# Token tiles of 480 columns in place of 416 in an attention and two-MLP kernel

## The chip, the core and the metric

The kernel runs on one core of a Trainium2 chip. The metric is the device time of one execution in microseconds (us), as the median of three runs. The engines are named as the profile names them: PE (TensorE, the matmuls), PEld (its weight loads, which run beside the matmuls), DVE (VectorE), ACT (ScalarE), POOL (GpSimd) and SP (SyncE, which issues most DMAs).

## The reference, cut to what matters

There are N = 12480 tokens of C = 128 channels and m = 32 inducing points. Two attentions follow each other, and then two MLPs with a hidden width of 2048. The outer function is the last one.

```python
def mab(q, kv):
    s = scale * (q @ kv.transpose(0, 2, 1))
    s = s - s.max(-1, keepdims=True)
    a = np.exp(s)
    a /= a.sum(-1, keepdims=True) + 1e-09
    return a @ kv
h = mab(I, x)
return mab(x, h).astype(np.float32)
...
h = x @ w_in
g = np.maximum(h, 0.0) + alpha * np.minimum(h, 0.0)
return (g @ w_out).astype(np.float32)
...
h = np.maximum(x @ w_in, 0.0)
return (h * h @ w_out).astype(np.float32)
```

`I` are the 32 inducing rows, which attend to all tokens; then each token attends to the 32 rows of `h`, and its result goes through the first MLP and the second, each 128 to 2048 to 128.

## The kernel before

**Stages.** The first attention reads all tokens once in its own tiles of 512 (`TILE1`) and a rest of 192; it needs every token before its result `hT` exists. Behind it the tokens are cut anew into `NT` = 30 tiles of `T` = 416. A tile is a matrix with channels (or 32 x 4 rows) on the partitions and its tokens on the columns, so every matmul behind the first attention has 416 moving columns, and every evacuation by ACT, DVE or POOL works on 128x416.

**Second attention.** `second_attention(tiles)` makes the softmax weights of the tokens for four tiles at once: the scores by four small matmuls (L449) side by side in one bank, then transposes, maximum, exponential and sum, and at the end a split into a rounded part and its remainder that DMAs spread over the partitions of `a_s`. Tile 0 goes alone, and its 416 tokens are cut into four pieces of 128 that overlap (`cuts`); tiles 1 to 3 come next, and from tile 4 on groups of four, with a last group of two. The steps of a group begin two tiles ahead of its first tile.

**Main loop.** A step `s` stands for one tile and one of 16 chunks of 128 hidden units; there are `total` = NT x 16 = 480 of them. In a step PE does ten matmuls in the reduced fp32 format (fp32r): `l1_a` one (L590, first MLP in; the attention's values are folded into the weights `w1s`), `l1_b` three (first MLP out; L600 to L602 are the three lines of the helper `three`, rounded and remainder parts), `l2_a` three (second MLP in) and `l2_b` three (second MLP out). `end_y1` adds one more matmul (L617) per tile. Each matmul has its own weight load. ACT evacuates `l1_a` (L594), `l2_a` (L632) and rounds the square (L640); DVE makes the remainder of the first (L596) and the square (L634); POOL makes the remainder of the square (L642), which DVE does in the last `LAG2` = 24 steps.

**Lags and fill.** `l1_b` runs 3 to 5 steps behind `l1_a`, `l2_a` 24 steps, `l2_b` 28 steps. So steps 0 to 23 hold only `l1_a` and `l1_b`. Into steps 0 to 40 the table `plan` and the list `PIECES` put the work that prepares weights: the inputs are 64-bit floats that come as pairs of 32-bit words and are turned into fp32 by ACT (L183, L186), DVE (L190, L194) and POOL (L195), then split into rounded and remainder parts (ACT L219 and L234, POOL L200), and a product of weights (`step_u`, 32 fp32 matmul records of 128 columns, L565).

**Order.** The instructions of an engine run in the order in which the code writes them; nothing is rearranged. What sets a step's work is the step number, never the width of a tile.

```python
    for s in range(total + LAG2 + LAG2B + 4):
        if s < total:
            l1_a(s, s < LAG2 and s % 2)
        if 0 <= s - LAG2 < total:
            l2_a(s - LAG2)
        if 0 <= s - LAG2 - 1 < total:
            l2_split(s - LAG2 - 1)
        ends = [(l1_b, i) for i in l1_b_at.get(s, [])]
```

Of the kernel before, what the change touches and what calls it, by code (L numbers as in the profile page):

```python
# [9 lines left out]
F32 = mybir.dt.float32  # L10
F32R = mybir.dt.float32r
I32 = mybir.dt.int32
U32 = mybir.dt.uint32
AF = mybir.ActivationFunctionType
ALU = mybir.AluOpType
AX = mybir.AxisListType


T = 416


TILE1 = (512, 128, 4)
# [2 lines left out]
Q = 4  # L25
# [3 lines left out]
def attention_then_two_mlps(ctx: ExitStack, tc, x, inducing, w_in, w_out, alpha, w2_in, w2_out, out):  # L29
# [15 lines left out]
    tiles1 = [(i * TILE1[0], *TILE1) for i in range(n1)] + [(n1 * TILE1[0], *REST1)]
# [3 lines left out]
    att = ctx.enter_context(tc.tile_pool(name="att", bufs=1))  # L49
# [7 lines left out]
    h2_bank = lambda: bank("h2", 2)  # L57
# [15 lines left out]
    f32 = lambda ap: ap.bitcast(F32)  # L73
# [40 lines left out]
    xT = keep_tile("xT", [P, N])  # L114

    def xt_cols(t):
        return xT[:, t * T : (t + 1) * T]

    w1s = keep_tile("w1s", [P, DFF], F32R)
    wo_hi = keep_tile("wo_hi", [P, NCH, P], F32R)  # L120
# [78 lines left out]
    def pool_lo(lo, a, hi):  # L199
        nc.gpsimd.tensor_tensor(lo, a, f32(hi), op=ALU.subtract)  # L200
# [155 lines left out]
    b = free_bank()  # L356
# [80 lines left out]
    def second_attention(tiles, cuts=None):  # L437

        nt = Q if cuts else len(tiles)
        n, w = nt * M, P if cuts else T
        v = {}

        def step_scores():
            b = v["s"] = free_bank()
            for i in range(nt):
                rhs = xt_cols(tiles[0])[:, cuts[i] : cuts[i] + w] if cuts else xt_cols(tiles[i])
                nc.tensor.matmul(  # L449
                    b[i * M : (i + 1) * M, :w], hT[:, :M], rhs, start=True, stop=True,  # L450
                    tile_position=(0, i * M),
                )

        def step_transpose():
            a = v["a"] = att.tile([P, T // M, M], F32, name="a2", tag="a2")
            v["a"] = a[:n, : w // M]
            nc.vector.transpose(a[:n].rearrange("p b j -> p (b j)")[:, :w], v["s"][:n, :w])

        def step_max():
            a = v["a"]  # L460
            mx = att.tile([P, T // M], F32, name="mx", tag="mx")[:n, : w // M]
            nc.vector.reduce_max(mx, a, axis=AX.X)
            nc.vector.tensor_tensor(a, a, mx.unsqueeze(2).to_broadcast([n, w // M, M]), op=ALU.subtract)

# [12 lines left out]
        def step_back():
            t = v["t"] = att.tile([P, T], F32, name="a2t", tag="a2t")
            nc.vector.transpose(t[:n, :w], v["a"].rearrange("p b j -> p (b j)"))

        def new_a_s(t):
            a_s[t] = att.tile([P, T], F32R, name="a_s", tag="a_s", bufs=5)
            return a_s[t]

        def step_split():

            hi = att.tile([P, T], F32R, name="a_hi", tag="a_hi")
            nc.scalar.copy(hi[:n], v["t"][:n])
            lo = att.tile([P, T], F32R, name="a_lo", tag="a_lo")
            pool_lo(lo[:n], v["t"][:n], hi[:n])  # L490
            for i, t in enumerate(tiles):
                d = new_a_s(t)
                for k in range(4):
                    nc.sync.dma_start(
                        out=f32(d[k * M : (k + 1) * M, :]),
                        in_=f32((lo if k % 2 else hi)[i * M : (i + 1) * M, :]),
                    )

        def step_spread():
            b = v["b"] = y1_bank()  # L500
            for i in range(nt):
                skip = max(0, cuts[i - 1] + w - cuts[i]) if i else 0
                nc.tensor.matmul(
                    b[:, cuts[i] + skip : cuts[i] + w], same_q[:, i, :], v["t"][:, skip:w], start=True, stop=True
                )

        def step_split_spread():

            d = a_s[tiles[0]] = new_a_s(tiles[0])[: 3 * M]
            nc.scalar.copy(d, v["b"][: 3 * M, :T])  # L510
            lo = d[M : 2 * M]
            nc.vector.tensor_tensor(lo, v["b"][M : 2 * M, :T], f32(lo), op=ALU.subtract)

        steps = [step_scores, step_transpose, step_max, step_exp, step_sum, step_back]
        return steps + ([step_spread, step_split_spread] if cuts else [step_split])
# [12 lines left out]
        else:  # L528
            nc.scalar.copy(dst, b)

    first = second_attention([0], [0, P, 2 * P, T - P])
    second = second_attention([1, 2, 3])
    first[0]()
    make_w1s(0)
# [51 lines left out]
    def l1_a(i, other_bank):  # L586
        t, c = divmod(i, NCH)
        b = h2_bank() if other_bank else h1_bank()
        a = a_s[t]
        nc.tensor.matmul(b[:, :T], w1s[: a.shape[0], c * P : (c + 1) * P], a, start=True, stop=True)  # L590

        tag = "g2" if i < EARLY and i % 2 else "g1"
        hi = wk.tile([P, T], F32R, name="g1h", tag=tag + "h", bufs=4)
        nc.scalar.activation(hi, b[:, :T], AF.Relu)  # L594
        lo = wk.tile([P, T], F32R, name="g1l", tag=tag + "l", bufs=4)
        nc.vector.scalar_tensor_tensor(lo, b[:, :T], 0.0, f32(hi), op0=ALU.max, op1=ALU.subtract)  # L596
        g1[i] = hi, lo

    def three(b, w_hi, w_lo, hi, lo, start, stop):
# [4 lines left out]
    def l1_b(i):  # L604
        t, c = divmod(i, NCH)
        if c == 0:
            y1_cur[t] = y1_bank() if t != 1 else y2_bank()
        b = y1_cur[t][:, :T]
        hi, lo = g1.pop(i)
        three(b, wo_hi[:, c, :], wo_lo[:, c, :], hi, lo, c == 0, False)  # L610
        if c == NCH - 1 and t:
            end_y1(t)

    def end_y1(t):
        b = y1_cur.pop(t)[:, :T]
        a = a_s.pop(t)
        nc.tensor.matmul(b, v_s[: a.shape[0]], a, start=False, stop=True)  # L617
        hi = wk.tile([P, T], F32R, name="y1h", tag="y1h", bufs=2)
        nc.scalar.copy(hi, b)  # L619
        lo = wk.tile([P, T], F32R, name="y1l", tag="y1l", bufs=2)  # L620
        nc.vector.tensor_tensor(lo, b, f32(hi), op=ALU.subtract)  # L621
        y1_split[t] = hi, lo

    def l2_a(i):
        t, c = divmod(i, NCH)
        b = h2_bank()[:, :T]
        cols = slice(c * P, (c + 1) * P)
        three(b, w2[0][:, cols], w2[1][:, cols], *y1_split[t], True, True)
        if c == NCH - 1:
            del y1_split[t]  # L630
        r = wk.tile([P, T], F32, name="r", tag="r", bufs=2)
        nc.scalar.activation(r, b, AF.Relu)  # L632
        sq = wk.tile([P, T], F32, name="sq", tag="sq", bufs=3)
        nc.vector.tensor_tensor(sq, b, r, op=ALU.mult)  # L634
        rr[i] = sq

    def l2_split(i):
        sq = rr.pop(i)
        hi = wk.tile([P, T], F32R, name="g2h", tag="g2h", bufs=4)
        nc.scalar.copy(hi, sq)  # L640
        lo = wk.tile([P, T], F32R, name="g2l", tag="g2l", bufs=4)
        (nc.vector if i >= total - LAG2 else nc.gpsimd).tensor_tensor(lo, sq, f32(hi), op=ALU.subtract)  # L642
        g2[i] = hi, lo

    def l2_b(i):
        t, c = divmod(i, NCH)
        if c == 0:
            y2_cur[t] = y2_bank()
        b = y2_cur[t][:, :T]
        hi, lo = g2.pop(i)  # L650
        cols = slice(c * P, (c + 1) * P)
        three(b, w2[2][:, cols], w2[3][:, cols], hi, lo, c == 0, c == NCH - 1)
        if c == NCH - 1:

            o = wk.tile([P, T], F32, name="o", tag="o", bufs=2)
            nc.vector.transpose(o, b)
            del y2_cur[t]
            dst = out[t * T : (t + 1) * T, :].rearrange("(b i) (a j) -> a i b j", i=M, j=M)
            for a in range(P // M):

                (nc.scalar if t == NT - 1 and a % 2 else nc.sync).dma_start(
                    out=dst[a], in_=o[a * M : (a + 1) * M, :].rearrange("i (b j) -> i b j", j=M)
                )
# [120 lines left out]
```

## Time and profile before

| | |
|---|---|
| time, median of 3 runs | 984.76 us (984.51 to 985.15) |
| span of the profiled execution, first to last instruction | 983.3 us |
| what lies around the span, against the median | 1.5 us |
| PE busy | 969.8 us (99%) |
| ACT busy | 769.2 us (78%) |
| DVE busy | 683.7 us (70%) |
| POOL busy | 555.3 us (56%) |
| mean granted TensorE clock | 0.995 of full speed |

The span is that of one execution taken by the profiler; the three times are of other executions. The busy share of PE is that of records that overlap, since a matmul begins before the one ahead of it has ended: what one matmul costs in a stream is the distance from its start to the next start.

### The profile page before, as it was taken

To read this page: it belongs to the slowest core of one execution; us is meant where nothing else is said; L and a number is where in the kernel's file an instruction comes from. 1 tells how busy PE (TensorE), PEld (TensorE's weight loads), DVE (VectorE), ACT (ScalarE), POOL (GpSimd) and SP (SyncE) were. 2 spreads that over 40 slices of the span, in tenths; PEclk is the share of its full clock that TensorE was granted. 3 is DMA by queue.
4 is the path that set the end of the run, shared out by engine and by line. 5 is a ranking of instruction groups with operands and counts; after the bars stand their busy time and mean duration, and the time that the engine had idled before them with its cause. 6 is when DMAs were issued, how large, how long until landed. Compare 5 with 4: busy or idle time off the path is not lost.

```text
span 983.3 us, 16104 instructions
## 1 busy us (share of the span) xinstructions
PE 969.8 (99%) x5353; PEld 941.0 (96%) x5353; DVE 683.7 (70%) x1204; ACT 769.2 (78%) x1600; POOL 555.3 (56%) x518
## 2 busy tenths in 40 slices
PE   9899999999999999999999999999999999999998
PEld 7578999999999999999999999999999999999997
DVE  5788876667766677666776667766677666766667
ACT  5689887778877787777787777877778777787776
POOL 2358865555655556555565555655556555565530
PEclk9989999999999999999999999999999999999999
DMA  9422001000010000100001000110001000010001
GB/s 331 146 90 66 10 11 34 10 10 10 14 31 10 10 9 17 29 10 10 9 19 27 10 9 10 25 21 10 9 9 29 17 10 10 10 27 1 10 9 19
DMA packets 66356, 28.42 MB, mean 29 GB/s; under 512 B 54224, under 2 KB 62176, under 8 KB 66272
## 3 DMA queue, kind: packets, MB, share of 16 engines
q1 hardware_dynamic: 65408, 27.28, 11.2%
q8 instruction: 42, 0.69, 0.3%
q14 instruction: 42, 0.34, 0.1%
q10 hardware_dynamic: 864, 0.11, 0.1%
HBM read 14.80 MB, written 6.39 MB: 22 GB/s over the span
## 4 chain that ended last, share of the span: by engine, by line
PE 93%; DVE 2%; ACT 2%; DMA 1%; issue 0%; SPq 0%; ACTq 0%; DVEq 0%
PE y L602 18%; PE y L601 18%; PE y L600 18%; PE h L602 9%; PE h L600 9%; PE h L601 9%; PE h L590 9%; DMA xg<-in_x_dram 1%; PE h L259 1%; ACT g1h L594 1%; PE ms L449 1%; PE y L617 1%; DVE g1l L596 0%; PE ms L273 0%; ACT aw L216 0%
## 5 line engine op out<-in xcount | busy, mean ns | idle before, releaser
L642 POOL TENSOR_TENSOR g2l<-sq,g2h 128x416 fp32r<-128x416 f32 x456 | 496.7, 1090 | 343.8 <-ACT g2h L640 208.0
L596 DVE SCALAR_TENSOR_TENSOR g1l<-h,g1h 128x416 fp32r<-128x416 f32 x480 | 282.5, 589 | 221.0 <-ACT g1h L594 216.3
L594 ACT ACTIVATE g1h<-h 128x416 fp32r<-128x416 f32 x480 | 248.3, 518 | 133.2 <-PE h L590 130.1
L634 DVE TENSOR_TENSOR sq<-h,r 128x416 f32<-128x416 f32 x480 | 283.5, 591 | 51.5 <-ACT r L632 5.0
L632 ACT ACTIVATE r<-h 128x416 f32<-128x416 f32 x480 | 249.1, 519 | 54.2 <-PE h L602 8.5
L640 ACT CAST g2h<-sq 128x416 fp32r<-128x416 f32 x480 | 255.3, 532 | 1.5 <-DVE sq L634 1.3
L590 PE MATMUL h<-a_s,w1s 128*128 128x416 f32 (+1 forms) x480 | 171.0, 358 | 3.1 <-DVE g1l L596 1.8
L602 PE MATMUL y<-g2l,w2o_hi 128*128 128x416 f32 x480 | 168.6, 351 | 0.0
L602 PE MATMUL y<-g1l,wo_hi 128*128 128x416 f32 x480 | 168.4, 351 | 0.0
L600 PE MATMUL h<-y1h,w2i_hi 128*128 128x416 f32 x480 | 168.0, 350 | 0.3 <-ACT y1h L619 0.2
L602 PE MATMUL h<-y1l,w2i_hi 128*128 128x416 f32 x480 | 167.9, 350 | 0.1
L601 PE MATMUL h<-y1h,w2i_lo 128*128 128x416 f32 x480 | 168.0, 350 | 0.0
L601 PE MATMUL y<-g1h,wo_lo 128*128 128x416 f32 x480 | 168.0, 350 | 0.0
L601 PE MATMUL y<-g2h,w2o_lo 128*128 128x416 f32 x480 | 167.9, 350 | 0.0
L600 PE MATMUL y<-g1h,wo_hi 128*128 128x416 f32 x480 | 167.8, 350 | 0.0
L600 PE MATMUL y<-g2h,w2o_hi 128*128 128x416 f32 x480 | 167.5, 349 | 0.0
L590 PEld LDWEIGHTS h<-a_s,w1s 128*128 128x128 f32 (+1 forms) x480 | 90.7, 189 | 12.0 <-DVE g1l L596 5.7
L600 PEld LDWEIGHTS h<-y1h,w2i_hi 128*128 128x128 f32 x480 | 90.0, 188 | 2.8 <-DVE sq L634 1.3
L600 PEld LDWEIGHTS y<-g1h,wo_hi 128*128 128x128 f32 x480 | 90.5, 188 | 1.0 <-issue 0.5
L601 PEld LDWEIGHTS y<-g2h,w2o_lo 128*128 128x128 f32 x480 | 90.1, 188 | 0.9 <-POOL w2o_lo L200 0.4
L601 PEld LDWEIGHTS y<-g1h,wo_lo 128*128 128x128 f32 x480 | 90.4, 188 | 0.5
L602 PEld LDWEIGHTS h<-y1l,w2i_hi 128*128 128x128 f32 x480 | 90.0, 188 | 0.7 <-DVE y1l L621 0.5
(124 smaller groups left out, 757.0 us busy)
## 6 DMA issues: line engine op xcount, KB each, us to landing
out_dram<-o SPq DMA_DIRECT2D x118, 52.0 KB, 1.9
xg<-in_x_dram SPq DMA_DIRECT2D x10, 512.0 KB, 9.3
raw<-in_moe_w_in_dram SPq DMA_DIRECT2D x8, 512.0 KB, 6.1
raw<-in_moe_w_out_dram SPq DMA_DIRECT2D x8, 512.0 KB, 4.1
a_s<-a_hi SPq DMA_DIRECT2D x58, 52.0 KB, 1.9
a_s<-a_lo SPq DMA_DIRECT2D x58, 52.0 KB, 1.9
xg<-in_x_dram SPq DMA_DIRECT2D x4, 256.0 KB, 3.5
out_dram<-o ACTq DMA_DIRECT2D x2, 52.0 KB, 2.4
```

The costliest lines, as they stand in the source:

```text
L259: nc.tensor.transpose(b[:, k * p : (k + 1) * p], x_t[g][:p, i, k, :], ident[:p, :p])
L449: nc.tensor.matmul(b[i * M : (i + 1) * M, :w], hT[:, :M], rhs, start=True, stop=True, tile_position=(0, i * M),)
L590: nc.tensor.matmul(b[:, :T], w1s[: a.shape[0], c * P : (c + 1) * P], a, start=True, stop=True)
L594: nc.scalar.activation(hi, b[:, :T], AF.Relu)
L596: nc.vector.scalar_tensor_tensor(lo, b[:, :T], 0.0, f32(hi), op0=ALU.max, op1=ALU.subtract)
L600: nc.tensor.matmul(b, w_hi, hi, start=start, stop=False)
L601: nc.tensor.matmul(b, w_lo, hi, start=False, stop=False)
L602: nc.tensor.matmul(b, w_hi, lo, start=False, stop=stop)
L632: nc.scalar.activation(r, b, AF.Relu)
L634: nc.vector.tensor_tensor(sq, b, r, op=ALU.mult)
L640: nc.scalar.copy(hi, sq)
L642: (nc.vector if i >= total - LAG2 else nc.gpsimd).tensor_tensor(lo, sq, f32(hi), op=ALU.subtract)
```

## The change

Behind the first attention the tokens are cut into 26 tiles of 480 instead of 30 of 416; both make 12480. The tile widths stand in a list `WIDTHS`, and every place that used `T` takes the width of its tile. The first attention keeps `TILE1`. The number of steps becomes 26 x 16 = 416; the lags, `plan` and `PIECES` keep their step numbers. Tile 0 of the second attention is cut at 0, 128, 256 and 352 instead of 0, 128, 256 and 288.

```diff
-T = 416
+WIDTHS = [(26, 480)]
+T = max(w for _, w in WIDTHS)
...
-    assert N % T == 0
-    NT = N // T
+    assert sum(n * w for n, w in WIDTHS) == N
+    wide = [w for n, w in WIDTHS for _ in range(n)]
+    first_token = [sum(wide[:t]) for t in range(len(wide) + 1)]
+    NT = len(wide)
...
-    groups = [list(range(a, min(a + Q, NT))) for a in range(0, NT, Q)]
+    groups, t = [], 0
+    for n, _ in WIDTHS:
+        groups += [list(range(a, min(a + Q, t + n))) for a in range(t, t + n, Q)]
+        t += n
...
-        return xT[:, t * T : (t + 1) * T]
+        return xT[:, first_token[t] : first_token[t + 1]]
...
-    first = second_attention([0], [0, P, 2 * P, T - P])
+    first = second_attention([0], [0, P, 2 * P, wide[0] - P])
...
-        a = a_s[t]
-        nc.tensor.matmul(b[:, :T], w1s[: a.shape[0], c * P : (c + 1) * P], a, start=True, stop=True)
+        a, w = a_s[t], wide[t]
+        nc.tensor.matmul(b[:, :w], w1s[: a.shape[0], c * P : (c + 1) * P], a, start=True, stop=True)
...
-        b = y1_cur[t][:, :T]
+        b = y1_cur[t][:, : wide[t]]
...
-            dst = out[t * T : (t + 1) * T, :].rearrange("(b i) (a j) -> a i b j", i=M, j=M)
+            dst = out[first_token[t] : first_token[t + 1], :].rearrange("(b i) (a j) -> a i b j", i=M, j=M)
```

On every engine the instructions keep their order; they become wider, and the later part of the program has fewer of them. On PE, where the main loop begins, these are the rows of before (L503 spreads the weights of tile 0 over the partitions, L590 is `l1_a`, L522 makes the weights `w1s`):

```order
L449 MATMUL ms<-xT,hT 32x416 x3
L389 MATMUL y_687<-ident,w_in_sb 128x128 x4
L522 MATMUL h_694<-w_in_sb,hT 128x512
L503 MATMUL y_707<-a2t,same_q 128x128 x3
L503 MATMUL y_707<-a2t,same_q 128x32
L590 MATMUL h_730<-a_s,w1s 128x416
L590 MATMUL h_741<-a_s,w1s 128x416
```

The same place on PE in the changed kernel, where the lines have moved by seven (L597 is `l1_a`):

```order
L456 MATMUL ms<-xT,hT 32x480 x3
L395 MATMUL y_687<-ident,w_in_sb 128x128 x4
L529 MATMUL h_694<-w_in_sb,hT 128x512
L510 MATMUL y_707<-a2t,same_q 128x128 x3
L510 MATMUL y_707<-a2t,same_q 128x96
L597 MATMUL h_730<-a_s,w1s 128x480
L597 MATMUL h_741<-a_s,w1s 128x480
```

No row has changed places; the fourth piece of tile 0 is 96 columns instead of 32, and the main loop's matmuls are 480 wide.

On POOL, the end of the program before (L642 is the remainder of the square, L475 and L200 belong to the last group of the second attention):

```order
L200 TENSOR_TENSOR a_lo<-a2t,a_hi 128x416
L642 TENSOR_TENSOR g2l<-sq,g2h 128x416 x56
L475 TENSOR_TENSOR a_11208<-a_11208,sm 64x416
L642 TENSOR_TENSOR g2l<-sq,g2h 128x416 x8
L200 TENSOR_TENSOR a_lo<-a2t,a_hi 64x416
L642 TENSOR_TENSOR g2l<-sq,g2h 128x416 x40
```

The same place on POOL in the changed kernel, where L652, L482 and L206 are those lines:

```order
L206 TENSOR_TENSOR a_lo<-a2t,a_hi 128x480
L652 TENSOR_TENSOR g2l<-sq,g2h 128x480 x56
L482 TENSOR_TENSOR a_9578<-a_9578,sm 64x480
L652 TENSOR_TENSOR g2l<-sq,g2h 128x480 x8
L206 TENSOR_TENSOR a_lo<-a2t,a_hi 64x480
L652 TENSOR_TENSOR g2l<-sq,g2h 128x480 x40
```

The counts of remainders between two attention steps (56, 8 and 40) are the same; ahead of this place the program has one cycle of four tiles less.

## Rows read from the trace of the kernel before

**Rows 1.** The page's first part: busy us, share of the span, instructions.

```profile
PE 969.8 (99%) x5353; PEld 941.0 (96%) x5353; DVE 683.7 (70%) x1204; ACT 769.2 (78%) x1600; POOL 555.3 (56%) x518
```

**Rows 2.** Windows: length, busy us of each engine (instructions), granted clock, DMA share, GB/s.

```profile
core 0: us, PE busy (x) PEld busy (x) DVE busy (x) ACT busy (x) POOL busy (x), PEclk, DMA share, GB/s
48.10:52.30 4.20, 2.90 (x5) 1.29 (x5) 4.08 (x7) 2.95 (x7) 3.33 (x3) 0.54 0.00 0
52.30:58.70 6.40, 6.29 (x14) 4.70 (x15) 5.90 (x12) 4.04 (x10) 2.71 (x3) 0.50 0.01 3
58.70:76.80 18.10, 17.49 (x102) 16.24 (x102) 13.71 (x24) 18.10 (x47) 10.41 (x9) 1.00 0.49 151
76.80:100.06 23.26, 22.69 (x114) 19.34 (x114) 19.29 (x33) 21.71 (x47) 21.18 (x17) 1.00 0.15 46
100.06:978.63 878.57, 878.53 (x4688) 867.84 (x4686) 608.30 (x1049) 691.56 (x1430) 503.65 (x466) 1.00 0.08 14
```

**Rows 3.** The last of these windows, the score matmuls L449 alone.

```profile
100.06:978.63 878.57, 5.42 (x44) 0.93 (x44) 1.00 0.08 14
```

**Rows 4.** Timeline of PE at 500 us, first and last of 51: start, us, instruction.

```profile
500.04 0.35 PE L590 MATMUL h<-a_s,w1s 128*128 128x416 f32 x1
...
509.42 0.35 PE L590 MATMUL h<-a_s,w1s 128*128 128x416 f32 x1
```

**Rows 5.** Timeline of PE at 57 us, where the granted clock is half.

```profile
57.39 0.55 PE L601 MATMUL y<-g1h,wo_lo 128*128 128x416 f32 x1
57.74 0.55 PE L602 MATMUL y<-g1l,wo_hi 128*128 128x416 f32 x1
58.08 0.55 PE L590 MATMUL h<-a_s,w1s 96*128 96x416 f32 x1
```

**Rows 6.** Timeline of PE, fp32 matmuls of 512 and of 128 columns.

```profile
41.39 0.59 PE L522 MATMUL h<-w_in_sb,hT 128*128 128x512 f32 x1
...
43.68 1.02 PE L522 MATMUL h<-w_in_sb,hT 128*128 128x512 f32 x2
...
66.56 1.05 PE L565 MATMUL y<-aw,wiT 128*128 128x128 f32 x8
```

**Rows 7.** Line L565: duration ns min/median/max, first and last start, form.

```profile
L565 PEld LDWEIGHTS y<-aw,wiT x32: 186/192/192, 66.4 to 72.5; 128*128 128x128 f32 x32
L565 PE MATMUL y<-aw,wiT x32: 270/275/377, 66.6 to 72.6; 128*128 128x128 f32 x32
```

**Rows 8.** Timeline of PE around the scores of one group of four tiles.

```profile
217.05 0.35 PE L602 MATMUL y<-g2l,w2o_hi 128*128 128x416 f32 x1
217.33 0.91 PE L449 MATMUL ms<-xT,hT 128*32 128x416 f32 x8
218.17 0.46 PE L590 MATMUL h<-a_s,w1s 128*128 128x416 f32 x1
218.47 0.35 PE L600 MATMUL h<-y1h,w2i_hi 128*128 128x416 f32 x1
```

**Rows 9.** The chain that ended last, 50 to 75 us: start, us, what.

```profile
50.46 1.29 DVE a L463
...
52.30 0.71 PE h L590
...
58.67 0.52 ACT g1h L594
...
74.34 0.43 ACT g1h L594
```

**Rows 10.** Groups by form, first 130 us: busy us, mean ns, idle before.

```profile
L596 DVE SCALAR_TENSOR_TENSOR g1l<-h,g1h 128x416 fp32r<-128x416 f32 x51 | 29.3, 581 | 10.1 <-ACT g1h L594 9.7
L642 POOL TENSOR_TENSOR g2l<-sq,g2h 128x416 fp32r<-128x416 f32 x25 | 28.9, 1168 | 6.4 <-ACT g2h L640 3.3 <-PE y L602 3.2
L594 ACT ACTIVATE g1h<-h 128x416 fp32r<-128x416 f32 x51 | 26.3, 524 | 5.6 <-PE h L590 5.3 <-PE y L601 0.2
...
L264 DVE COPY xT<-h 128x512 f32<-128x512 f32 x12 | 7.9, 688 | 4.0 <-PE h L259 3.8
...
L200 POOL TENSOR_TENSOR w2o_lo<-wf,w2o_hi 128x512 fp32r<-128x512 f32 x4 | 5.7, 1414 | 1.0 <-ACT w2o_hi L234 1.0
...
L529 ACT CAST w1s<-y 128x512 fp32r<-128x512 f32 x2 | 1.2, 586 | 2.0 <-PE y L522 2.0
```

**Rows 11.** Timeline of the end: last matmul and the transpose behind it.

```profile
978.14 0.45 PE L602 MATMUL y<-g2l,w2o_hi 128*128 128x416 f32 x1
978.63 0.62 DVE L656 STREAM_TRANSPOSE o<-y 128x416 f32<-128x416 f32 x1 [0.55 <-PE y L602]
```

More of the change, by code (lines that the diff above doesn't have):

```diff
@@ L441, in second_attention @@
         nt = Q if cuts else len(tiles)
-        n, w = nt * M, P if cuts else T
+        tw = wide[tiles[0]]
+        n, w = nt * M, P if cuts else tw
         v = {}
@@ L481, in new_a_s @@
         def new_a_s(t):
-            a_s[t] = att.tile([P, T], F32R, name="a_s", tag="a_s", bufs=5)
+            a_s[t] = att.tile([P, T], F32R, name="a_s", tag="a_s", bufs=5)[:, : wide[t]]
             return a_s[t]
@@ L487, in step_split @@
             hi = att.tile([P, T], F32R, name="a_hi", tag="a_hi")
-            nc.scalar.copy(hi[:n], v["t"][:n])
+            nc.scalar.copy(hi[:n, :w], v["t"][:n, :w])
             lo = att.tile([P, T], F32R, name="a_lo", tag="a_lo")
-            pool_lo(lo[:n], v["t"][:n], hi[:n])
+            pool_lo(lo[:n, :w], v["t"][:n, :w], hi[:n, :w])
             for i, t in enumerate(tiles):
@@ L494, in step_split @@
                     nc.sync.dma_start(
-                        out=f32(d[k * M : (k + 1) * M, :]),
-                        in_=f32((lo if k % 2 else hi)[i * M : (i + 1) * M, :]),
+                        out=f32(d[k * M : (k + 1) * M]),
+                        in_=f32((lo if k % 2 else hi)[i * M : (i + 1) * M, :w]),
                     )
@@ L509, in step_split_spread @@
             d = a_s[tiles[0]] = new_a_s(tiles[0])[: 3 * M]
-            nc.scalar.copy(d, v["b"][: 3 * M, :T])
+            nc.scalar.copy(d, v["b"][: 3 * M, :tw])
             lo = d[M : 2 * M]
-            nc.vector.tensor_tensor(lo, v["b"][M : 2 * M, :T], f32(lo), op=ALU.subtract)
+            nc.vector.tensor_tensor(lo, v["b"][M : 2 * M, :tw], f32(lo), op=ALU.subtract)
         steps = [step_scores, step_transpose, step_max, step_exp, step_sum, step_back]
@@ L588, in l1_a @@
         b = h2_bank() if other_bank else h1_bank()
-        a = a_s[t]
-        nc.tensor.matmul(b[:, :T], w1s[: a.shape[0], c * P : (c + 1) * P], a, start=True, stop=True)
+        a, w = a_s[t], wide[t]
+        nc.tensor.matmul(b[:, :w], w1s[: a.shape[0], c * P : (c + 1) * P], a, start=True, stop=True)
         tag = "g2" if i < EARLY and i % 2 else "g1"
[L593 to L596, printed above, removed]
+        hi = wk.tile([P, T], F32R, name="g1h", tag=tag + "h", bufs=4)[:, :w]
+        nc.scalar.activation(hi, b[:, :w], AF.Relu)
+        lo = wk.tile([P, T], F32R, name="g1l", tag=tag + "l", bufs=4)[:, :w]
+        nc.vector.scalar_tensor_tensor(lo, b[:, :w], 0.0, f32(hi), op0=ALU.max, op1=ALU.subtract)
         g1[i] = hi, lo
@@ L614, in end_y1 @@
     def end_y1(t):
-        b = y1_cur.pop(t)[:, :T]
+        w = wide[t]
+        b = y1_cur.pop(t)[:, :w]
         a = a_s.pop(t)
         nc.tensor.matmul(b, v_s[: a.shape[0]], a, start=False, stop=True)
-        hi = wk.tile([P, T], F32R, name="y1h", tag="y1h", bufs=2)
+        hi = wk.tile([P, T], F32R, name="y1h", tag="y1h", bufs=2)[:, :w]
         nc.scalar.copy(hi, b)
-        lo = wk.tile([P, T], F32R, name="y1l", tag="y1l", bufs=2)
+        lo = wk.tile([P, T], F32R, name="y1l", tag="y1l", bufs=2)[:, :w]
         nc.vector.tensor_tensor(lo, b, f32(hi), op=ALU.subtract)
@@ L625, in l2_a @@
         t, c = divmod(i, NCH)
-        b = h2_bank()[:, :T]
+        w = wide[t]
+        b = h2_bank()[:, :w]
         cols = slice(c * P, (c + 1) * P)
@@ L630, in l2_a @@
             del y1_split[t]
-        r = wk.tile([P, T], F32, name="r", tag="r", bufs=2)
+        r = wk.tile([P, T], F32, name="r", tag="r", bufs=2)[:, :w]
         nc.scalar.activation(r, b, AF.Relu)
-        sq = wk.tile([P, T], F32, name="sq", tag="sq", bufs=3)
+        sq = wk.tile([P, T], F32, name="sq", tag="sq", bufs=3)[:, :w]
         nc.vector.tensor_tensor(sq, b, r, op=ALU.mult)
@@ L638, in l2_split @@
         sq = rr.pop(i)
-        hi = wk.tile([P, T], F32R, name="g2h", tag="g2h", bufs=4)
+        w = wide[i // NCH]
+        hi = wk.tile([P, T], F32R, name="g2h", tag="g2h", bufs=4)[:, :w]
         nc.scalar.copy(hi, sq)
-        lo = wk.tile([P, T], F32R, name="g2l", tag="g2l", bufs=4)
+        lo = wk.tile([P, T], F32R, name="g2l", tag="g2l", bufs=4)[:, :w]
         (nc.vector if i >= total - LAG2 else nc.gpsimd).tensor_tensor(lo, sq, f32(hi), op=ALU.subtract)
@@ L648, in l2_b @@
             y2_cur[t] = y2_bank()
-        b = y2_cur[t][:, :T]
+        w = wide[t]
+        b = y2_cur[t][:, :w]
         hi, lo = g2.pop(i)
@@ L653, in l2_b @@
         if c == NCH - 1:
-            o = wk.tile([P, T], F32, name="o", tag="o", bufs=2)
+            o = wk.tile([P, T], F32, name="o", tag="o", bufs=2)[:, :w]
             nc.vector.transpose(o, b)
             del y2_cur[t]
-            dst = out[t * T : (t + 1) * T, :].rearrange("(b i) (a j) -> a i b j", i=M, j=M)
+            dst = out[first_token[t] : first_token[t + 1], :].rearrange("(b i) (a j) -> a i b j", i=M, j=M)
             for a in range(P // M):
```

## Prediction

> **What bounds the kernel now.** I read the page first: PE is busy 99% of the span, ACT 78%, POOL 56% [rows 1]. The windows then split the program in two at 100.06 us, the start of step 35. Behind it lie 878.6 us in which PE has no gap (878.53 of 878.57 busy) and no other engine is busy more than 79% [rows 2]. Ahead of it, from the first main-loop matmul at 48.1 us, lie 52.0 us of fill, and there the bound changes: DVE (4.08 of 4.20), then PE at half clock (6.29 of 6.40 at 0.50), then ACT (18.10 of 18.10), then a mixture in which POOL is busy 21.18 and ACT 21.71 of 23.26 us. So the change is worth two things: what a matmul costs beyond its columns in the long stage, and how far fixed work in the fill hides the wider tiles.
>
> The long stage is a pure stream. It holds 4688 PE records, 44 of them scores [rows 3], so 4644 wide matmuls. In the timeline 50 of them take 9.38 us, 187.6 ns each [rows 4]. At full clock (2.4 GHz) 416 columns are 173.3 ns. So a matmul costs some 14 ns more than its columns. At half clock the distance is 345 ns (57.39 to 58.08 for two), and 416 columns at 1.2 GHz are 346.7 ns: there the extra is gone [rows 5]. Something of about that length per matmul runs beside the columns when these are slow and sticks out when they are fast.
>
> **The change part by part: the long stage.** The columns stay what they were (12480 tokens, ten matmuls and one per tile), but the matmuls become fewer: 480 x 10 + 30 = 4830 before, 416 x 10 + 26 = 4186 after, so 644 less. All 644 go from the long stage, since the fill is the same steps: 4000 are left there.
>
> What is the extra, fixed or growing with the columns? No row shows an fp32r matmul of another width, so this is the disputed price. For fp32 matmuls two widths are there. Two records of 512 take 1.02 us, one lasts 0.59, so they start 0.43 apart, against 2 x 512 / 2.4 = 0.427; eight of 128 take 1.05, one lasts 0.275 [rows 6, 7], so the distance is 0.775 / 7 = 0.111, against 0.107. The extra is 3 to 4 ns at either width: where it can be seen at two widths, it is a price per matmul, not per column. By that I take the 14 ns as fixed. From below it is bounded by 3.5 ns fixed, the fp32 rows' own, with the rest growing by the columns, and by nothing fixed at all.
>
> The Trainium skill ("TensorE: Matmul & The Clock Gate", section "Back-to-back issue gap") gives columns / 2.4 + 2.5 ns at full clock and columns / 1.2 at half. The trace agrees at half clock (345 ns) and for the fp32 matmuls, not for the fp32r stream, which has 187.6 ns where the rule has 175.8. If only those 2.5 ns were fixed, 644 matmuls less would save 1.6 us; by my reading they save 9.3.
>
> The scores of a group of four stretch two distances from 0.38 to 1.42 us (217.05 to 218.47), so they cost 1.04 us [rows 8]; with 64 columns more in four passes (256 / 2.4 = 107 ns) 1.15. The long stage has six such groups before, five after.
>
> Before: (878.6 - 6 x 1.04 - 0.5 at the end) / 4644 = 187.7 ns, so 14.4 beyond the columns. After: 200 + 14.4 = 214.4 ns; 4000 x 0.2144 = 857.6, with 5 x 1.15 and 0.5 it is 863.8. **Term 1: -14.8 us.** The engines beside PE don't come near: a step becomes 2.14 us long, and POOL's one remainder per step about 1.33 (below).
>
> **The fill.** The same steps 0 to 34 now carry 15.4% more columns, but the conversions, the splits of the weights and the fp32 products keep their sizes. The prices of 64 columns more come from the 416-wide and the 512-wide groups of each engine [rows 10]: ACT (586 - 524) / 96 x 64 = 41 ns, DVE (688 - 581) / 96 x 64 = 71 ns, POOL (1414 - 1168) / 96 x 64 = 164 ns. These compare different operations, so they are estimates. The chain says whose time counts in each stretch: DVE to 52.3, PE to 58.7, ACT to 74 us [rows 9].
> - To 48.1: the spread and split of tile 0 stand ahead of the first L590: 64 columns more in the fourth spread, two passes each in two records (0.11), and one ACT and one DVE operation: +0.2.
> - 48.1 to 52.3: five of DVE's seven operations are 416 wide: +0.4.
> - 52.3 to 58.7, PE at half clock: 14 records, two of them 512-wide L522, so 12 x 64 / 1.2 = 53 ns: +0.6.
> - 58.7 to 76.8, ACT: steps 8 to 23 with one L594 each, and two other wide operations, 18 x 41 ns: +0.7. PE's own growth lies beneath: it has 102 records there, 34 of them fp32, and 68 x 27 ns = 1.8 us fits into its waits.
> - 76.8 to 100.06: nine of POOL's 17 operations are wide, 9 x 164 ns: +1.5. PE alone would need (114 - 8) x 0.2144 + 1.15 = 23.9, so +0.6 is the least; 15.4% of the stretch (+3.6) the most.
>
> **Term 2: +3.4 us**, between +2 and 15.4% of all 52.0 us (+8.0).
>
> **The end.** Behind the last matmul come the transpose, 0.62 us [rows 11], which grows by 0.07, and output DMAs with 15% more bytes: **+0.15**. The drain of 24 steps is part of term 1; DVE makes both its operations there, and I read its pace from the same stage, in which PE has no gap.
>
> Other edits cost nothing that shows. The second attention's operations are wider but run two tiles ahead of their use, now 32 steps of 2.14 us instead of 1.88; were that cover gone, one group's chain of some ten operations would stand open, and nothing in the long stage shows it near. There are 16 DMAs less to spread `a_s` and 16 less to the output; SP has nothing else to do by then. No step passes another on any queue, so no new wait is added; whoever waited for a 416-wide evacuation waits 40 to 160 ns longer, with lags of 3 to 5 steps around it.
>
> Sum: -14.8 + 3.4 + 0.15 = -11.2. The profiled span goes from 983.3 to 972.1; the median lies 1.5 above the span and keeps that: 984.8 - 11.2 = **973.6 us**.
>
> **The rivals.**
> - *The extra grows with the columns.* With 3.5 ns fixed a matmul takes (187.7 - 3.5) x 480 / 416 + 3.5 = 216.0 ns, 4000 of them 864.0; term 1 is -8.4 and the time 980.0. With nothing fixed, 216.6 ns: term 1 -6.0, time 982.3. For it speaks that fp32 rows show so small a fixed part, against it that the extra vanishes at half clock. The skill's rule named above, 2.5 ns fixed, falls between the two (216.2 ns).
> - *The weight load sets the pace.* PEld is busy 96% [rows 1]. If loads and columns shared one stream, 128 + 416 columns in 187.7 ns, then 128 + 480 take 209.8: 839.2, time about 955. If the load alone took 187 ns, 480 columns (203.5 with 3.5) would just pass it: time about 930. Against both: L565 has a load for each matmul and a pair every 111 ns [rows 7], and half clock shows columns alone.
> - *The clock stays low* (slower). It is about half (0.54 and 0.50) from 48.1 to 58.7 us, where PE is gappy at first and then almost without gaps [rows 2]. If it came back only behind the ACT stretch, PE would need 68 x 400 + 34 x 222 ns (twice 111) = 34.7 us there instead of the 18.8 forecast: +15.9, time about 989.5. It decides from 70% of that stretch on. Against it: PE's order is the same and its matmuls are wider, so it is busier ahead of the rise, not less.
> - *The whole fill grows as PE does*: +8.0, time 978.2, the upper end of my own case.
>
> **How the numbers follow.** My case 0.62 (its own range 972 to 978); extra that grows 0.22; load 0.08; clock 0.05; others 0.03. The range 970.5 to 983.0 takes in the first two. A measurement of this kernel tells about 0.2%, 2 us, from no change, so faster means below 982.8: nearly all of my case, the load, and most of the second, 0.84; the rest of the second, where the fill costs more than forecast, and half-way clocks: same 0.09; slower 0.07.
>
> **What would show it.** In the profile after, fifty matmuls of the long stage should take 10.72 us (10.80 to 10.83 if the extra grows, under 10.5 if the load counts). Step 35 should begin at 103.5 us, and PE's gapless stage from there last 863.8. The half clock should end near 60 us. The prediction is wrong if the distance isn't 214, or if step 35 begins beyond 108 us.

## The result and the profile after

The changed kernel takes 990.78 us (median of 4 runs, 989.65 to 991.67) against 984.92 for the kernel before in the same comparison: a ratio of 1.0056, 95% interval 1.0042 to 1.0070. It is slower by 5.9 us, where 11.2 us less was forecast. The profiled run took 989.65 us, the fastest of the four, with a span of 987.9.

The first part of the page after shows that PE is still the bound, while its loads and every other engine have more room than in [rows 1].

```profile
PE 973.2 (99%) x4701; PEld 821.2 (83%) x4701; DVE 663.6 (67%) x1061; ACT 742.5 (75%) x1402; POOL 539.8 (55%) x452
```

The windows after, cut at the same steps as [rows 2] (length, busy us of each engine with its instructions, granted clock, DMA share, GB/s):

```profile
47.80:52.09 4.29, 1.78 (x6) 0.86 (x6) 4.19 (x7) 3.08 (x7) 3.47 (x3) 1.00 0.00 0
52.09:57.43 5.34, 5.00 (x12) 3.25 (x13) 5.13 (x10) 4.15 (x9) 2.75 (x3) 0.68 0.00 0
57.43:76.89 19.46, 19.38 (x104) 16.56 (x103) 16.77 (x27) 19.04 (x47) 10.52 (x9) 1.00 0.50 147
76.89:102.51 25.62, 25.19 (x114) 19.55 (x113) 21.09 (x34) 23.66 (x48) 22.39 (x18) 1.00 0.15 42
102.51:983.00 880.49, 880.39 (x4036) 750.20 (x4034) 584.13 (x906) 661.81 (x1231) 486.59 (x399) 1.00 0.07 14
```

The last of these windows, the scores (L456) alone, answers to [rows 3]:

```profile
102.51:983.00 880.49, 5.05 (x36) 0.78 (x36) 1.00 0.07 14
```

Step 35 begins at 102.51 us, 2.45 later than before, so the fill as a whole cost less than forecast (+3.4). The long stage holds 4036 - 36 = 4000 wide matmuls, exactly the number forecast, and PE has no gap in it. But it lasts 880.5 us and not 863.8. The timeline shows why (start, us, instruction; first and last of 51, as in [rows 4]):

```profile
500.77 0.38 PE L597 MATMUL h<-a_s,w1s 128*128 128x480 f32 x1
...
511.69 0.38 PE L597 MATMUL h<-a_s,w1s 128*128 128x480 f32 x1
```

Fifty matmuls take 10.92 us, 218.4 ns each, where 214.4 was forecast. Over the stage it is (880.4 - 5 x 1.15 - 0.5) / 4000 = 218.5 ns, 18.5 beyond the 200 ns of the columns instead of 14.4. That is 4.1 ns x 4000 = 16.4 us, nearly the whole miss of 17.2. The new distance is more than 480 / 416 times the old one (216.6): between these two kernels the extra neither stayed fixed nor grew in step with the columns, it grew faster.

### The profile page after: what moved, and what is told of

Its sections match the earlier page's. It is cut to its first block, busy times and chain, and to the rows that moved or that the text cites. A ratio compares the mean times of both kernels' runs of the same rounds, so it can differ in the third digit from the quotient of the medians.

```text
span 987.9 us, 14140 instructions
## 1 busy us (share of the span) xinstructions
PE 973.2 (99%) x4701; PEld 821.2 (83%) x4701; DVE 663.6 (67%) x1061; ACT 742.5 (75%) x1402; POOL 539.8 (55%) x452
## 3 DMA queue, kind: packets, MB, share of 16 engines
q1 hardware_dynamic: 64256, 27.23, 11.2%
## 4 chain that ended last, share of the span: by engine, by line
PE 96%; DVE 2%; ACT 1%; DMA 1%; issue 0%; SPq 0%; ACTq 0%
PE y L607 18%; PE y L609 18%; PE y L608 18%; PE h L607 9%; PE h L609 9%; PE h L608 9%; PE h L597 9%; PE h L265 1%; PE ms L279 1%; PE ms L456 1%; PE y L625 1%; DMA xg<-in_x_dram 1%; PE y L340 1%; PE y L572 0%; PE y L331 0%
## 5 line engine op out<-in xcount | busy, mean ns | idle before, releaser
L652 POOL TENSOR_TENSOR g2l<-sq,g2h 128x480 fp32r<-128x480 f32 x392 | 481.2, 1228 | 358.9 <-ACT g2h L650 358.9
L603 DVE SCALAR_TENSOR_TENSOR g1l<-h,g1h 128x480 fp32r<-128x480 f32 x416 | 272.2, 655 | 240.9 <-ACT g1h L601 235.4
L601 ACT ACTIVATE g1h<-h 128x480 fp32r<-128x480 f32 x416 | 238.0, 573 | 155.3 <-PE h L597 154.4
L643 DVE TENSOR_TENSOR sq<-h,r 128x480 f32<-128x480 f32 x416 | 273.1, 656 | 56.2 <-ACT r L641 6.2
L641 ACT ACTIVATE r<-h 128x480 f32<-128x480 f32 x416 | 238.5, 573 | 64.5 <-PE h L609 13.0
L650 ACT CAST g2h<-sq 128x480 fp32r<-128x480 f32 x416 | 243.7, 586 | 0.9 <-DVE sq L643 0.9
L597 PE MATMUL h<-a_s,w1s 128*128 128x480 f32 (+1 forms) x416 | 160.1, 386 | 4.3 <-DVE g1l L603 2.5
L609 PE MATMUL y<-g2l,w2o_hi 128*128 128x480 f32 x416 | 158.9, 382 | 0.0
L607 PE MATMUL y<-g2h,w2o_hi 128*128 128x480 f32 x416 | 158.8, 382 | 0.0
L607 PE MATMUL y<-g1h,wo_hi 128*128 128x480 f32 x416 | 158.7, 382 | 0.0
L597 PEld LDWEIGHTS h<-a_s,w1s 128*128 128x128 f32 (+1 forms) x416 | 78.0, 188 | 23.7 <-DVE g1l L603 5.6
L607 PEld LDWEIGHTS h<-y1h,w2i_hi 128*128 128x128 f32 x416 | 78.1, 188 | 14.4 <-DVE sq L643 0.6
```

Source lines behind the costliest of these rows:

```text
L597: nc.tensor.matmul(b[:, :w], w1s[: a.shape[0], c * P : (c + 1) * P], a, start=True, stop=True)
L601: nc.scalar.activation(hi, b[:, :w], AF.Relu)
L603: nc.vector.scalar_tensor_tensor(lo, b[:, :w], 0.0, f32(hi), op0=ALU.max, op1=ALU.subtract)
L607: nc.tensor.matmul(b, w_hi, hi, start=start, stop=False)
L609: nc.tensor.matmul(b, w_hi, lo, start=False, stop=stop)
```

## The experiments

All distances are from start to start in a stream of fp32r matmuls; "extra" is what lies beyond columns / 2.4. The wider kernels all derive from the changed one.

### Five widths in one kernel

```diff
-WIDTHS = [(26, 480)]
+WIDTHS = [(8, 416), (8, 480), (3, 448), (4, 512), (5, 384)]
```

Expected: 

> Same program, but the tiles behind the first attention have five widths one after another: 8 of 416, 8 of 480, 3 of 448, 4 of 512, 5 of 384 tokens, all in buffers of 512 columns. Read is the distance from matmul to matmul of each width in the stream. Theory W (the extra belongs to the width): 416 has 187.6 ns and 480 has 218.5 as in the two kernels, 448 lies between at 202 to 203, 512 at 233 to 235, 384 at 172 to 174. Theory B (the buffers' place or pitch of 1920 bytes does it): with a pitch of 2048 bytes 480 falls to 214 and 512 has 227 to 228. Theory L (the weight load of 187 ns holds up 416): 384 stays at 187 and does not fall to 174.

Measured: 990.02 us in one run. The timeline of PE, two rows for each of the widths 416, 480, 448, 512 and 384, each pair from a stretch where all ten matmuls of a step have that width:

```profile
240.50 0.35 PE L597 MATMUL h<-a_s,w1s 128*128 128x416 f32 x1
...
249.83 0.35 PE L597 MATMUL h<-a_s,w1s 128*128 128x416 f32 x1
...
500.71 0.38 PE L597 MATMUL h<-a_s,w1s 128*128 128x480 f32 x1
...
511.55 0.38 PE L597 MATMUL h<-a_s,w1s 128*128 128x480 f32 x1
...
629.80 0.36 PE L597 MATMUL h<-a_s,w1s 128*128 128x448 f32 x1
...
639.80 0.36 PE L597 MATMUL h<-a_s,w1s 128*128 128x448 f32 x1
...
741.78 0.40 PE L597 MATMUL h<-a_s,w1s 128*128 128x512 f32 x1
...
751.15 0.39 PE L597 MATMUL h<-a_s,w1s 128*128 128x512 f32 x1
...
873.00 0.34 PE L597 MATMUL h<-a_s,w1s 128*128 128x384 f32 x1
...
880.07 0.34 PE L597 MATMUL h<-a_s,w1s 128*128 128x384 f32 x1
```

Five, five, five, four and four steps of ten matmuls give 186.6, 216.8, 200.0, 234.2 and 176.8 ns. The extras from 384 to 512 columns, in order of width, are 16.8, 13.3, 13.3, 16.8 and 20.9 ns. They go down and up with the width, so theory W falls as a rule of growing extra, and theory L falls because 384 lies under 187. Theory B had its figures wrong too (214 and 227 expected), but so had W at four of the five widths, 480 among them: 216.8 ns here against 218.5 in the changed kernel. What stands out is that 416 and 448 have only 13.3 beyond their columns, less than the narrower 384 has.

### Matmuls alone, behind the kernel

```diff
+    for width in (512, 480, 448, 416, 384, 352, 320):
+        for _ in range(30):
+            o, w_, x_, first, last_ = stream(width, 0)
+            nc.tensor.matmul(o, w_, x_, start=first, stop=last_)
+    for width, pitch in ((480, 480), (480, 512), (416, 416), (416, 480)):
+        for k in range(30):
+            o, w_, x_, first, last_ = stream(width, k % 4 * pitch)
...
```

Expected: 

> The changed kernel with matmuls added behind its last one, with no other engine at work and results that nobody reads: 30 each at 512, 480, 448, 416, 384, 352 and 320 columns, then 30 each at 480 and 416 columns whose moving operand starts at multiples of 480, 512, 416 and 480 columns. Theory W: 480 has 218 to 219 ns here too and 416 187 to 188, whatever the start. Theory N (the other engines' reads and writes of the same memories do it): alone 480 falls to 213 to 214 and 416 to 186.7 (13.3 beyond the columns for both). Theory B: the distance changes with the start of the moving operand. Theory L: 384, 352 and 320 all stay at 187.

Measured: the first rows of the groups of 30 in the timeline of PE; a group's length is the distance to the next one's first row.

```profile
990.23 0.38 PE L780 MATMUL h<-w2o_hi,w2i_lo 128*128 128x480 f32 x1
...
996.73 0.36 PE L780 MATMUL y<-w2o_hi,w2i_lo 128*128 128x448 f32 x1
...
1002.81 0.35 PE L780 MATMUL h<-w2o_hi,w2i_lo 128*128 128x416 f32 x1
...
1008.41 0.33 PE L780 MATMUL h<-w2o_hi,w2i_lo 128*128 128x384 f32 x1
...
1018.46 0.31 PE L780 MATMUL h<-w2o_hi,w2i_lo 128*128 128x320 f32 x1
...
1022.86 0.38 PE L784 MATMUL h<-w2o_hi,w2i_lo 128*128 128x480 f32 x1
...
1029.32 0.38 PE L784 MATMUL y<-w2o_hi,w2i_lo 128*128 128x480 f32 x1
```

480 takes 6.50 / 30 = 216.7 ns, 448 202.7, 416 186.7, 320 146.7. With no other engine at work 480 doesn't fall to 213, so theory N falls (its 186.7 for 416 came true, but 416 has that in the run of five widths too, beside the other engines); 320 runs at 146.7, so the load doesn't hold 416 up (theory L). And 480 with the moving operand at multiples of 480 columns takes 215.3 ns (6.46 / 30), 416 at multiples of 416 or of 480 columns 188.1: the same width has another distance at other places.

### Other buffers, same widths

The changed kernel in buffers of 512 and of 496 columns, and the kernel before in buffers of 480:

```diff
-T = max(w for _, w in WIDTHS)
+T = 512
```

Expected for 480 in 512: 

> The changed kernel with every buffer behind the first attention 512 columns long, of which 480 are used: pitch 2048 bytes instead of 1920, and other addresses. Theory B: distance 214 ns and about 973 us. Theories W and N: 218.5 ns and 990 to 991 us.

Expected for 416 in 480: 

> The kernel before (30 tiles of 416) in buffers of 480 columns: pitch 1920 bytes instead of 1664. Theory B: distance about 190 to 192 ns instead of 187.6 and 1000 us or more. Theories W, N and L: 187.6 ns and 984 to 986 us.

Expected for 480 in 496: 

> The changed kernel in buffers of 496 columns, pitch 1984 bytes. Theory P: a third distance, neither 218.6 (pitch 1920) nor 216.7 (pitch 2048) but anywhere between 213.3 and 221, with the time following it by 4 us per ns. A rule that the shorter pitch is worse: 217 to 218.6. Theory W: 218.6 or 216.7.

Measured: 480 in 512 takes 982.0 us, ratio 0.9974 to the kernel before (0.9962 to 0.9985). Only the buffers differ from the changed kernel's 990.78. 416 in 480 takes 984.8 (ratio 1.000, 0.999 to 1.0009), 480 in 496 takes 990.53 in one run. The timelines of the first and of the last of these three, 50 matmuls each:

```profile
501.52 0.38 PE L597 MATMUL h<-a_s,w1s 128*128 128x480 f32 x1
...
512.35 0.38 PE L597 MATMUL h<-a_s,w1s 128*128 128x480 f32 x1
```

```profile
500.01 0.38 PE L597 MATMUL h<-a_s,w1s 128*128 128x480 f32 x1
...
510.90 0.38 PE L597 MATMUL h<-a_s,w1s 128*128 128x480 f32 x1
```

In 512 it is 216.6 ns, in 496 217.8 (a mean of 218.4 over the stage). So the pitch of the buffers and where they lie move the time by 9 us. A pitch of 1920 bytes does not cost by itself: at 416 columns it changes nothing. The run in 496 decides little: the third distance that theory P expected did not come out clearly, since time and mean distance are those of the pitch of 1920 bytes. The addresses in the built programs show what differs: all fp32r weights of the main loop but `v_s` start at 160 bytes modulo 256. The moving operands start at 64 and 192 in turn with pitch 1664 or 1920, always at 64 with pitch 2048, and at 0, 64, 128 and 192 with pitch 1984.

### The place of either operand

```diff
+    for k in range(16):
+        twenty(480, 16 * k, 0)
+    for k in range(16):
+        twenty(480, 0, P * k)
+    for k in range(16):
+        twenty(480, 0, 16 * k)
...
```

`twenty(width, moving, weights)` is 20 matmuls with the moving operand and the weights so many columns into their tensors, which both start at 160 bytes modulo 256.

Expected: 

> The changed kernel with 67 groups of 20 matmuls added behind its last one, nothing else at work and results that nobody reads. First 16 groups of 480 columns whose moving operand starts 0, 64, ... 960 bytes into its tensor, weights fixed; then 16 with the weights moved by 512 bytes each; 16 with the weights moved by 64 bytes each; 3 with another place in the output bank; 8 of 416 and 8 of 512 columns with the moving operand moved by 128 bytes each. Theory P (moving operand and weights collide by their places in memory): the distance at 480 columns changes with the start of either, between about 213.3 (13.3 beyond the columns) and 220, and not with the output. Theory W (the width alone): 216.7 in every group of 480, 186.7 at 416, 226.7 at 512.

Measured, in the timeline of PE (start and us of a group of 20): moving operand moved by 0, 64, 128 and 192 bytes, and by 384 and 448; then weights moved by 0, 64 and 128 bytes; then 512 columns with the moving operand moved by 0 and 128.

```profile
983.10 4.49 PE L773 MATMUL h<-w2o_hi,w2i_hi 128*128 128x480 f32 x20
987.43 4.52 PE L773 MATMUL y<-w2o_hi,w2i_hi 128*128 128x480 f32 x20
991.79 4.53 PE L773 MATMUL h<-w2o_hi,w2i_hi 128*128 128x480 f32 x20
996.15 4.48 PE L773 MATMUL y<-w2o_hi,w2i_hi 128*128 128x480 f32 x20
...
1009.18 4.56 PE L773 MATMUL h<-w2o_hi,w2i_hi 128*128 128x480 f32 x20
1013.58 4.49 PE L773 MATMUL y<-w2o_hi,w2i_hi 128*128 128x480 f32 x20
...
1122.05 4.49 PE L773 MATMUL h<-w2o_hi,w2i_hi 128*128 128x480 f32 x20
1126.38 4.49 PE L773 MATMUL y<-w2o_hi,w2i_hi 128*128 128x480 f32 x20
1130.70 4.52 PE L773 MATMUL h<-w2o_hi,w2i_hi 128*128 128x480 f32 x20
...
1234.65 4.72 PE L773 MATMUL y<-w2o_hi,w2i_hi 128*128 128x512 f32 x20
1239.20 4.82 PE L773 MATMUL h<-w2o_hi,w2i_hi 128*128 128x512 f32 x20
```

The distances from the first to the next group's start are 216.5, 218, 218 and 216.3 ns for the moving operand and repeat for larger offsets every 256 bytes, but with 220.0 at 128 in the later repeats (384, 640 and 896 bytes). The weights moved by 64 and 192 bytes give the values of the moving operand at 192 and 64 (216.0, 218.5): it is the one place against the other that counts. Weights moved by 512 bytes (16 groups) and another place in the output bank (3 groups) change nothing. At 512 columns it is 227.5 against 233 with the first matmuls, 226.7 and 233.6 once settled. At 416 columns the repeat fails: offsets of 0, 256, 512 and 768 bytes settle at 186.5, 188.3, 188.3 and 186.5 ns, those of 128, 384, 640 and 896 at 186.7, 189.7, 190.5 and 186.7. Theory W falls. Theory P holds in that the place counts; that it counts modulo 256 bytes is shown at 480 and 512 columns alone. The expected minimum of 213.3 was not reached at 480.

A finer grid, in steps of 32 bytes at five widths (`for width in (480, 512, 416, 448, 384)`, `twenty(width, 8 * k, 0)`):

Expected: 

> 40 groups of 20 matmuls behind the changed kernel, alone, at 480, 512, 416, 448 and 384 columns, the moving operand moved in steps of 32 bytes from 0 to 224. Theory P: each width has its own row of distances that depends on the offset; 480 lies between 216 and 220.5 and nowhere at 213.3, 512 between 226.7 and 233.6, and 416 stays under 190.

Measured: 480 at 128 and 160 bytes, 416 at 0, 32 and 64, same view.

```profile
1000.84 4.43 PE L773 MATMUL h<-w2o_hi,w2i_hi 128*128 128x480 f32 x20
1005.11 4.52 PE L773 MATMUL y<-w2o_hi,w2i_hi 128*128 128x480 f32 x20
...
1055.31 3.90 PE L773 MATMUL h<-w2o_hi,w2i_hi 128*128 128x416 f32 x20
1059.05 4.03 PE L773 MATMUL y<-w2o_hi,w2i_hi 128*128 128x416 f32 x20
1062.91 3.94 PE L773 MATMUL h<-w2o_hi,w2i_hi 128*128 128x416 f32 x20
```

Settled (the mean from the fifth matmul of a group on, as in what follows), 480 has 216.7, 219.9 and 213.3 ns at 0, 32 and 128 bytes, 416 has 186.5 and 193.3 at 0 and 32. Over all eight places 384 lies between 173.3 and 176.8, 416 between 186.5 and 193.3, 448 between 200.0 and 206.7, 480 between 213.3 and 220.0, 512 between 226.7 and 234.1. Two expectations failed: 480 does reach 213.3, at 128 bytes, where the run before had 217.8 at the very same addresses and 220.0 at 256, 512 and 768 bytes more; and 416 goes over 190. So a place has more than one settled distance. Between the two groups at the same addresses only what ran ahead of them differs; the run with shorter loads below begins with the same 16 groups of 480 and 512 in the same order and repeats their distances to within 0.3 ns.

### A shift alone, in the kernel

One unused tile ahead moves all moving operands and nothing else of the stream:

```diff
     att = ctx.enter_context(tc.tile_pool(name="att", bufs=1))
+    att.tile([128, 32], F32, name="gap", tag="gap")
```

480 in buffers of 512, shifted by 128 bytes. Expected: 

> The 480-wide kernel in buffers of 512 columns, with one unused tile of 128 bytes per partition put ahead, so that every moving operand lies 128 bytes further; pitch and everything else as in the unshifted run (982.0 us, 216.7 ns). By the program's addresses the moving operands then start 32 bytes behind the weights modulo 256 instead of 160. Theory P (place of the moving operand against the weights): the half of the 1920-byte pitch that lies there must have cost about 220.5 ns (2 x 218.6 - 216.7), so the whole stream falls to 219 to 221.5 ns and the time rises to 992 to 1000 us. Theory W or a rule of the pitch alone: 216.7 ns, 982 us.

24 tiles of 512 and one of 192 (`WIDTHS = [(24, 512), (1, 192)]`), not shifted. Expected: 

> 24 tiles of 512 tokens and one of 192, no shift: moving operands 160 bytes behind the weights modulo 256, where 512 columns were near 233.7 ns in the run of five widths. Theory P: 233 to 234 ns, about 993 us. Theory W: the same. A fixed 14.4 ns for each matmul, as in the prediction: 227.7 ns and about 970 us.

The same, shifted by 96 bytes (`[128, 24]`), so that the places agree. Expected: 

> The same 24 tiles of 512 and one of 192, with one unused tile of 96 bytes ahead, so that moving operands and weights have the same place modulo 256. Theory P: 226.7 ns in the stream as in the group measured alone at that place, and about 967 us, faster than both kernels. Theory W or a rule of the pitch alone: no change against the unshifted 512, 233 to 234 ns and about 993 us.

Measured, the timelines of the three in this order, the first of them at two times:

```profile
222.00 0.38 PE L598 MATMUL h<-a_s,w1s 128*128 128x480 f32 x1
...
232.89 0.38 PE L598 MATMUL h<-a_s,w1s 128*128 128x480 f32 x1
...
239.52 1.01 PE L457 MATMUL ms<-xT,hT 128*32 128x480 f32 x8
...
500.80 0.38 PE L598 MATMUL h<-a_s,w1s 128*128 128x480 f32 x1
...
511.80 0.38 PE L598 MATMUL h<-a_s,w1s 128*128 128x480 f32 x1
```

```profile
501.12 0.39 PE L597 MATMUL h<-a_s,w1s 128*128 128x512 f32 x1
...
512.83 0.40 PE L597 MATMUL h<-a_s,w1s 128*128 128x512 f32 x1
```

```profile
500.63 0.39 PE L598 MATMUL h<-a_s,w1s 128*128 128x512 f32 x1
...
509.70 0.39 PE L598 MATMUL h<-a_s,w1s 128*128 128x512 f32 x1
```

480 shifted: 50 matmuls in 11.00 us from 500.80 on, 220.0 ns, and 994.31 us (ratio 1.0093, 1.0078 to 1.0108) where the unshifted one has 982.0. 512 unshifted: 50 in 11.71, 234.2 ns, and 996.86 us (1.0126, 1.0109 to 1.0142). 512 shifted: 40 in 9.07, 226.8 ns, and 971.02 us (0.9860, 0.9844 to 0.9876). 96 unused bytes per partition are worth 25.8 us. Theory P gave all three distances to within 1 ns for most of the stream (the times at 512 lie 4 us above its figures). But the stream of 480 ran at 217.8 ns up to 239 us (10.89 us for 50 matmuls from 222.00 on), under the 219 expected, and changed to 220.0 behind the score matmuls that start at 239.52 us, at the same places: modulo 256 bytes no address differs between the two stretches. At 512 the two streams agree with the groups alone at these places (226.7 with equal places, 234.1 at 160 bytes), so the other engines, whose buffers the tile moves too, are not needed to explain them. The last kernel beats the kernel before by 1.4% and the changed one by 2.0%.

### Shorter loads, and the kernel before at another place

Groups of 20 alone with weights of 128, 64 and 32 columns (`w2[0][:, :m]`). Expected: 

> 48 groups of 20 matmuls behind the changed kernel, alone: weights of 128, of 64 and of 32 columns, each at 480 and 512 moving columns, the moving operand moved in steps of 32 bytes from 0 to 224. Theory P1 (what collides with the moving operand is the reading of the next weights): with weights of 32 columns, a quarter of the reading, the extra beyond the columns and its spread over the places shrink clearly, at 512 columns from 13 to 21 ns to under 10 everywhere. Theory P2 (the moving operand's own reading depends on its place, whatever the load does): the same rows of 216 to 220 and 226.7 to 234 at 32 columns of weights.

Measured, 480 columns with weights of 32 columns at 0, 32 and 64 bytes, same view:

```profile
1128.11 4.56 PE L773 MATMUL h<-w2o_hi,w2i_hi 128*32 128x480 f32 x20
1132.51 4.48 PE L773 MATMUL y<-w2o_hi,w2i_hi 128*32 128x480 f32 x20
1136.82 4.44 PE L773 MATMUL h<-w2o_hi,w2i_hi 128*32 128x480 f32 x20
```

480 settles at 220.1, 215.6 and 213.3 ns. Over all eight places weights of 32 columns give 213.3 to 220.1 ns at 480 and 230.9 to 239.9 at 512, weights of 64 columns 215.3 to 219.9 and 226.7 to 232.0. The extra does not shrink with a quarter of the weights, whose load takes 108 ns instead of 188 (P1 falls), but it is not the same row either (P2 falls as written): other places are good and bad.

The kernel before in buffers of 512, shifted by 128 bytes. Expected: 

> The kernel before (30 tiles of 416) in buffers of 512 columns and shifted by 128 bytes, so that all moving operands start 32 bytes behind the weights modulo 256; alone, 416 columns had 193.3 ns at that place, 186.5 to 190 at most others. Theory P: up to 193.3 ns in the stream and up to 1010 us; the 187.6 ns of the kernel before was one place among several. Theory W: 187.6 ns and 985 us.

Measured: 981.59 us, ratio 0.9978 (0.9959 to 0.9998), with 60 matmuls in 11.20 us:

```profile
500.84 0.35 PE L598 MATMUL h<-a_s,w1s 128*128 128x416 f32 x1
...
512.04 0.35 PE L598 MATMUL h<-a_s,w1s 128*128 128x416 f32 x1
```

It is 186.7 ns, 13.4 beyond the columns. The 193.3 ns of the group alone at this place did not come back in the stream; the time went down instead of up. Theory P in the form "the group alone tells the stream" fails at 416. Two things were changed at once here, the buffers and the shift; the run of five widths has 416 in buffers of 512 without the shift, at 186.6 ns. So at 416 the shift changes nothing in the stream, and the gain goes with the buffers, in which all moving operands have one place, where the kernel before has two in turn. Why two places cost 416 a nanosecond is not shown. At 384 the group alone misses too: 173.3 ns at 160 bytes, 176.8 in the stream at that place.

## Why the prediction was wrong

**The bound and the counts** held, and the sum of the fill came near. PE has no gap in the long stage, 4000 matmuls are left in it, and step 35 begins 2.45 us later against +3.4 forecast. In part that is luck. The half clock did not end near 60 us; it is gone before 57.5 (0.68 in the window to 57.43, 1.00 behind it), and the window from 47.8 to 52.1 ran at full clock, where [rows 2] have 0.54. So the stretch for which +0.6 was forecast became 1.06 us shorter (6.40 to 5.34), and the two behind it grew by 3.7 us (18.10 to 19.46 and 23.26 to 25.62) where 2.2 were forecast. That the change shortened the half clock is not shown: the mean granted clock lies between 0.993 and 0.998 over the executions of the kernel before and between 0.994 and 0.997 over those of the changed one, of which the profiled one has the highest. The other engines' wider operations cost +55 ns on ACT (573 against 518 on the pages), +66 on DVE (655 against 589) and +138 on POOL (1228 against 1090), for 41, 71 and 164 forecast. The end, from the last transpose at 982.93 us on, costs 987.9 - 982.9 = 5.0 us against 4.7, +0.3 for +0.15. The median lies 2.9 us above the profiled span, not 1.5, since the profiled execution was the fastest.

**The step that failed** is "By that I take the 14 ns as fixed" in term 1. The 14.4 ns were read at one width and at one set of places, and carried to another width on the word of fp32 matmuls, whose extra of 3 to 4 ns is another quantity. The runs show two parts in it. About 13.3 ns were the least that settled at six of the seven widths from 320 to 512 columns (146.7, 173.3, 186.5, 200.0, 213.3, 226.7 ns; 352 had one group alone, at 161); that part is fixed, as forecast. On top come 0 to 8 ns with full weights that depend on the width, on where the moving operand starts against the weights (modulo 256 bytes at 480 and 512 columns), and on what ran ahead. The kernel before had 1 ns of them, the changed kernel 5.2. Term 1 measured 982.93 - 102.51 - 878.57 = +1.85 us instead of -14.8; 13.3 + 200 ns would have been worth another 4.4 us on top of the forecast.

**The rivals.** The extra that grows with the columns was nearest, but its 216.0 to 216.6 ns were passed, and the run with five widths shows no growth with the columns (448 has less extra than 384). The load as the pace falls at 146.7 ns. The clock that stays low did the opposite in the profiled execution. None of the prediction's cases held that the same width could have more than one distance, and so the range ended at 983.0. The rule of the Trainium skill that the prediction weighed ("TensorE: Matmul & The Clock Gate", section "Back-to-back issue gap") is stated there for isolated matmuls, and no fp32r stream here meets it: the least extra is 13.3 ns, not 2.5.

**What stays open.** That the place counts at 480 and 512 is shown by shifts that move nothing else of PE's stream (982.0 to 994.3 us at 480, 996.9 to 971.0 at 512). Why it counts, and that anything collides, is not shown: the other engines are not needed for it, and a shorter weight load doesn't take it away, though it makes other places good and bad. Nor is it known which of its distances a stream settles in, since 480 alone at 128 bytes modulo 256 gave 213.3, 217.8 and 220.0, the shifted stream of 480 changed from 217.8 to 220.0 on its way, and 384 and 416 in the kernel went against the group measured alone. The 218.5 ns of the changed kernel, whose moving operands start at two places in turn, lie at the mean of the two streams that have one of these places each (216.6 and 220.0 ns); but the 187.6 of the kernel before lie above both of its own (186.6 and 186.7), and why is open too.

## What to carry to other kernels

In a PE-bound stream of fp32r matmuls, read the distance from start to start before any change of width, and read it for the new width from a run; one width's overhead cannot be carried to another. Where the distance lies more than some 14 ns beyond columns / 2.4, try moving the streamed buffers by 32 to 128 bytes against the weights: an unused tile of 96 bytes was worth 2.6% here, more than the change of tile size. A change that only resizes buffers moves every later address too, so compare it at several shifts, in the kernel itself, before calling the size good or bad.

## What the runs showed of the hardware that I had not expected

- The distance of 512-column fp32r matmuls is 226.8 or 234.2 ns in programs that differ by a shift of 96 bytes; alone, it is 226.7 with equal places modulo 256 and 233.6 with 128 bytes between.
- 480 columns at one place modulo 256 bytes can settle at 213.3, 217.8 or 220.0 ns with nothing else at work, and one stream changed from 217.8 to 220.0 ns behind eight score matmuls.
- fp32r matmuls at full clock have some 13 ns or more beyond their columns at every width tried, where fp32 matmuls have 3 to 4 (0.111 us against 0.107 in [rows 6]) and at half clock fp32r ones have none [rows 5].
- Weights of 32 columns don't shorten the distance, though their load takes 108 ns instead of 188: 480 columns still take 213.3 to 220.1 ns.
